# Joining the transposing transfers of a fused attention and highway layer, with the schedule made anew

## The chip, the cores and the metric

The kernel runs on one core of a Trainium2 chip. The metric is the device time of one execution in microseconds (us). The five engines are named as in the profile: PE (matmuls; PEld its weight loads), DVE, ACT, POOL, and SP, which here only issues DMA transfers. A name with a q (SPq, POOLq) is the engine's sequencer, which issues and waits.

## The reference

```python
# q, k, v: 8 batches, 12 heads, 448 rows, 64 columns, float32; tau = 0.1
q_n = q / (norm(q) + 1e-06);  k_n = k / (norm(k) + 1e-06)      # per row
scores = q_n @ k_n.T / tau
attn = softmax(scores)
x = (attn @ v), heads side by side                             # 3584 x 768
H = maximum(x @ w_h, 0);  T = sigmoid(x @ w_t + b_t)           # 768 x 768 weights
out = T * H + (1 - T) * x
```

## The kernel before

The work goes over 8 batches. Within one, the 12 heads are taken as 6 pairs (heads p and p + 6), so there are 48 pairs, numbered `s = 6 * b + p`. The 448 rows of a head are 3 x 128 main rows and a tail of 64. Operands of products are f16.

For each batch the main rows of q, k and v are loaded with a cast by POOL (`load_main`, `load_v`), the f32 tails by SP (`load_tails`). `square`, `tail_squares` and `folds` make the squared norms; `newton` makes their inverse roots (on ACT in batch 0, in seven small DVE steps later). `scaled` multiplies q and k of one pair by the roots into a buffer `qn`, on POOL (line 499); `qtnorm` and `ktnorm` scale the tails into `qtn` and `kb`.

The products need q and k with the 64 columns on the partitions, so `qn` is transposed into `qT`. In batches 0 to 3 `turn` does that with seven PE transposes and one eviction by DVE (line 547). In batches 4 to 7 (`BY_DMA`) it is a transposing DMA transfer that SP issues: one per pair, six 128 x 128 blocks (line 532). `turn_tails` does the same for the tails: one transfer of three blocks for q (`qtT`, line 555) and one of six for k (`kbT`, line 558).

`scores` makes the score products of a pair on PE (lines 600 and 614) and ACT takes their exponential (606, 618). `attend` multiplies with v (644, 648, 664), and DVE divides by the row sums (672, 674) into `x`, a buffer of one batch. v is cast into `vp` by `vcast` (626) and `vtcast` (632).

`ffn` is the highway layer, four tiles a batch: three of 128 x 2 rows and one half tile of the tails, in which the two halves of the 768 columns lie on the two halves of the partitions. x of a tile is transposed, in batches 1 to 6 by one transfer from SP for each tile (line 704). The products with both weights are lines 745 and 729, the gate is made by ACT (768, 769) and DVE (782, 787, 790), the last addition by POOL (line 795) and at the end by DVE. SP stores the result: one transfer of a full tile (805), two for the half tile, 64 rows of half the columns each (801).

The order is written out by hand. Every operation is put down with its engine, what it reads and what it writes; `ORDER` is the order in which all 1723 of them are issued, and so the order on each engine, and `SLOTS` says which buffer of a ring each new value takes. Nothing else schedules. `NR` gives the rings: four `qn`, four `qT`, three `xT`, four `os` (results that wait for their store).

DVE and POOL are kept apart by extra order: an operation that uses the port that both share is marked `port`. Such an operation on POOL waits for the last such one before it on DVE; those in `URGENT` are also waited for by the next one on DVE.

SP issues in order. Its transfers use eight completion marks in turn, so that a transfer also waits until the one eight before it has landed.

Of the kernel before, what the change touches and what calls it, by code (L numbers as in the profile page):

```python
# [9 lines left out]
FP16 = mybir.dt.float16  # L10
# [92 lines left out]
""".replace("\n", "")  # L103
)

URGENT = frozenset(
    int(n)
    for n in """
116 135 154 155 225 310 336 337 394 413 485 583 621 736 774 811 877 945 963 998 1080 1106 1140 1147 1166 1237
1268 1283 1298 1369 1387 1405 1440 1471 1553 1554 1571 1589 1590 1607 1608 1643 1691  # L110
""".split()
)


class Op:
# [801 lines left out]
```

## Time and profile before

| | |
|---|---|
| median of 3 runs (lowest to highest) | 275.48 us (273.61 to 279.13) |
| the profiled execution | 274.65 us |
| its span in the profile | 272.8 us |
| granted TensorE clock | 0.994 |
| DMA traffic | 43.13 MB in 104249 packets |

The span is what the profile shows from the first instruction to the last; the time of the execution is 1.85 us longer. Durations of single instructions come from that one execution. Of two instructions in a row on an engine, the second often starts about 0.1 us before the first ends, so summed durations exceed busy time by a few per cent.

### The profile page before, as it was taken

What the parts mean: (1) busy time and instruction counts of PE and PEld (TensorE: products, weight loads), DVE (VectorE), ACT (ScalarE), POOL (GpSimd) and SP (SyncE); (2) the same over time, 40 slices, a digit from 0 to 9 for tenths busy, and PEclk for the clock granted to TensorE, in tenths of its full rate; (3) what the DMA queues carried; (4) which work ended last, traced back from release to release, by engine and by line L of the source; (5) the groups of instructions that cost most, each with busy time, mean ns of one, the idle gap of its engine ahead of it and who ended that gap; (6) DMA issues with size and microseconds to landing.
All of it is one profiled execution on the core that took longest, in us unless ns stands there. A gap on an engine that the chain in (4) does not pass through costs nothing.

```text
span 272.8 us, 9106 instructions
## 1 busy us (share of the span) xinstructions
PE 243.6 (89%) x3783; PEld 163.2 (60%) x3783; DVE 198.2 (73%) x446; ACT 209.6 (77%) x312; POOL 159.1 (58%) x172
## 2 busy tenths in 40 slices
PE   0467898999999999999999897998899999999990
PEld 0235475766775676666656574665566767677650
DVE  6577989999989889976876778629853454446464
ACT  2479999879896998789689898797798995683120
POOL 5979656585584775576766564558667464300540
PEclk9999999999999999999999999999999999999997
DMA  7999999999859999996999989999795749620243
GB/s 131 221 192 191 180 207 202 186 194 198 105 78 176 209 164 119 150 171 128 210 157 151 173 191 181 143 190 222 173 167 86 116 124 191 204 90 2 60 178 113
DMA packets 104249, 43.13 MB, mean 158 GB/s; under 512 B 98064, under 2 KB 101136, under 8 KB 104208
## 3 DMA queue, kind: packets, MB, share of 16 engines
q0 software_dynamic: 38464, 16.32, 49.3%
q1 hardware_dynamic: 64512, 25.80, 48.7%
q8 instruction: 30, 0.49, 0.7%
q10 hardware_dynamic: 1232, 0.43, 0.6%
q14 instruction: 11, 0.09, 0.1%
HBM read 37.82 MB, written 11.01 MB: 179 GB/s over the span
## 4 chain that ended last, share of the span: by engine, by line
PE 53%; DVE 17%; DMA 14%; ACT 5%; POOL 3%; issue 3%; SPq 2%; POOLq 0%; ACTq 0%; DVEq 0%
PE pS L745 24%; PE pS L600 7%; PE pB L648 7%; PE pS L729 4%; DMA qT<-qn 4%; DMA qr<-in_q_dram 4%; DMA out_dram<-os 3%; PE pB L664 3%; PE pB L614 3%; PE pB L644 3%; DVE sq L374 2%; POOL qn L499 2%; DMA kr<-in_k_dram 2%; DVE f L388 2%; ACT E L606 2%
## 5 line engine op out<-in xcount | busy, mean ns | idle before, releaser
L606 ACT ACTIVATE E<-pS 128x896 f16<-128x896 f32 x144 | 128.5, 920 | 21.0 <-PE pS L600 18.0
L745 PEld LDWEIGHTS <-xT 64*128 64x128 f16 x1152 | 52.9, 94 | 33.6 <-issue 2.2
L795 POOL TENSOR_TENSOR os<-x,hm 128x768 f32<-128x768 f16 (+1 forms) x30 | 44.2, 1479 | 41.6 <-DVE hm L790 28.5
L745 PE MATMUL pS<-wt,xT 64*128 64x384 f16 x576 | 58.6, 323 | 0.6 <-DMA xT<-x 0.6
L745 PE MATMUL pS<-wh,xT 64*128 64x384 f16 x576 | 57.5, 323 | 0.0
L499 POOL TENSOR_TENSOR qn<-kr,rs 128x384 f16<-128x384 f16 x47 | 39.1, 841 | 30.4 <-DVE rd L672 10.4
L499 POOL TENSOR_TENSOR qn<-qr,rs 128x384 f16<-128x384 f16 x47 | 38.9, 832 | 22.9 <-DVE hm L790 8.3
L600 PE MATMUL pS<-qT 64*128 64x384 f16 x288 | 44.1, 327 | 3.8 <-DMA qT<-qn 1.7
L648 PE MATMUL pB<-vp,E 128*128 128x65 f16 x864 | 43.6, 194 | 0.0
L782 DVE SCALAR_TENSOR_TENSOR hm<-pS,x 128x768 f16<-128x768 f32 (+1 forms) x33 | 27.4, 833 | 19.8 <-PE pS L745 13.6
L648 PEld LDWEIGHTS <-E 128*128 128x128 f16 x864 | 38.5, 98 | 1.2 <-issue 0.7
L600 PEld LDWEIGHTS <-qT 64*128 64x128 f16 x576 | 23.2, 94 | 21.7 <-issue 7.8
L644 PE MATMUL pB<-vp,Et 128*128 128x130 f16 x144 | 32.0, 222 | 0.8 <-ACT Et L618 0.6
L769 ACT ACTIVATE tt<-pS 128x768 f16<-128x768 f32 x24 | 19.5, 813 | 16.3 <-PE pS L745 15.0
L618 ACT ACTIVATE Et<-pB 128x512 f16<-128x512 f32 x48 | 28.5, 603 | 2.9 <-PE pB L614 2.7
L674 DVE SCALAR_TENSOR_TENSOR x<-pB,rd 128x448 f16<-128x448 f32 x48 | 29.7, 620 | 1.1
L600 PE MATMUL pS<-qtT,qT 64*128 64x64 f16 x282 | 27.6, 189 | 0.0
L672 DVE RECIPROCAL rd<-pB 128x7 f32<-128x7 f32 x48 | 9.5, 200 | 22.7 <-PE pB L648 14.4
L280 PE MATMUL pB<-fill 128*128 128x384 f16 x40 | 9.6, 367 | 13.3 <-DVE fill L251 10.7
L626 ACT COPY vp<-vr 128x384 f16<-128x384 f16 x42 | 21.1, 515 | 0.0
L790 DVE TENSOR_TENSOR hm<-tt,hm 128x768 f16<-128x768 f16 (+1 forms) x32 | 18.3, 581 | 2.8 <-POOL os L795 2.6
L664 PE MATMUL pB<-vp,E 128*128 128x65 f16 x288 | 18.3, 194 | 0.2 <-DVE x L674 0.2
(95 smaller groups left out, 382.3 us busy)
## 6 DMA issues: line engine op xcount, KB each, us to landing
out_dram<-os SPq DMA_DIRECT2D x24, 384.0 KB, 3.7
vr<-in_v_dram POOLq DMA_DIRECT2D x8, 576.0 KB, 9.6
kr<-in_k_dram POOLq DMA_DIRECT2D x7, 576.0 KB, 9.8
qr<-in_q_dram POOLq DMA_DIRECT2D x7, 576.0 KB, 11.4
qt<-in_q_dram SPq DMA_DIRECT2D x16, 96.0 KB, 5.8
vt<-in_v_dram SPq DMA_DIRECT2D x16, 96.0 KB, 5.0
out_dram<-os SPq DMA_DIRECT2D x16, 96.0 KB, 2.4
kt<-in_k_dram SPq DMA_DIRECT2D x14, 96.0 KB, 4.9
```

What stands on the lines that cost most here:

```text
L499: return e.tensor_mul(R("qn", s)[:, t].rearrange("l c ab d -> l ab c d"), rows(t, b, p, p + 1)[:, :, 0, :].rearrange("l ab (c d) -> l ab c ...
L600: ins = nc.tensor.matmul(dst, lhsT=qT[ln, 384 + 128 * c : 512 + 128 * c], rhs=rhs, start=True, stop=True)
L606: return nc.scalar.activation(R("E", s)[:, c, :, 0:448], R("S", 3 * s + c)[:, :, 0:448], AF.Exp, scale=inv_tau)
L618: op("ACT", f"expt {s}", lambda: nc.scalar.activation(R("Et", s)[:, 64:576], R("B", ("S", s))[:, :], AF.Exp, scale=inv_tau), key + 3, r=[( ...
L626: return nc.vector.tensor_copy(dst, src) if b == 0 else nc.scalar.copy(dst, src)
L644: nc.tensor.matmul(U[:, 2 * c : 2 * c + 2, :].rearrange("p g e -> p (g e)"), lhsT=Et[:, 128 + 128 * c : 256 + 128 * c], rhs=vp[:, 6:8, :]. ...
L648: ins = nc.tensor.matmul(U[:, 2 * c + ab, :], lhsT=EF[:, j, 576 * ab + 128 * c : 576 * ab + 128 * c + 128], rhs=vp[:, 3 * ab + j, :], star ...
L664: ins = nc.tensor.matmul(U[:, 6, :], lhsT=lt, rhs=rh, start=(n == 0), stop=(n == 7))
L674: op("DVE", f"ev {s}", lambda: nc.vector.scalar_tensor_tensor(out=R("x", b)[:, :, D * p : D * p + D], in0=U_()[:, :, 0:D], scalar=0.0, in1 ...
L745: ins = nc.tensor.matmul(P[:, h, 0:MH], lhsT=lt, rhs=rh, start=(part == 0 and cc == (-1 if wi == 0 else 0)), stop=(part == 1 and cc == CC ...
L782: return nc.vector.scalar_tensor_tensor(out=o_, in0=i0, scalar=0.0, in1=xs, op0=ALU.max, op1=ALU.subtract)
L795: op(en, f"out{wd} {g}", lambda: eng.tensor_add(R("os", g)[:, 0:W], xall(), R("hm", g)[:, 0:W]), at + 0.1, r=[("gg", g), ("x", b)], w=[("o ...
```

## The change

The transposing transfers are joined. In batches 4 to 7, `qn` and `qT` hold two pairs, and one transfer of twelve blocks turns q and k of both. The scaled tails of q now lie behind those of k in `kb`, and one transfer of nine blocks turns both (`tT` in place of `qtT` and `kbT`). x of a batch is turned by two transfers, of twelve and nine blocks, in place of four. The two half stores of a tail tile become one, whose destination is written as 2 x 64 x 384. SP has 36 operations fewer (108 in place of 144).

The rings follow: two `qn` of two pairs each, three `qT` of two, two `xT` of two tiles, two `sq` in place of three. Order and slots are new lists throughout, so that every engine's order changes, the first loads included. In the list of POOL the small first loads of k and q come in another order, and the bias loads stand between them.

A set `MOVED` lists 131 operations that run on another engine than the one that the code names first: `pick` chooses. The moves by kind:

| operation | from | to | count |
|---|---|---|---|
| scaling of q and k (`scaled`) | POOL | DVE | 45 |
| last addition (`out`, `outh`) | POOL | DVE | 14 + 4 |
| scaling of q tails (`qtnorm`) | POOL | DVE | 5 |
| scaling of k tails (`ktnorm`) | DVE | POOL | 10 |
| cast of v (`vcast`) | ACT to DVE, DVE to ACT | | 20, 2 |
| cast of v tails (`vtcast`) | ACT | DVE | 4 |
| squares (`square`, `tail_squares`) | DVE to ACT, ACT to DVE | | 15, 6 |
| eviction after PE transposes (`cpT`) | DVE | ACT | 6 |

PE has the same instructions, in another order. The diff without the lists, shortened:

```diff
-    NR = dict(qr=3, kr=3, qt=2, kt=2, kb=2, vr=3, vt=2, vp=2, sq=3, f1=2, f2=2, n2=2, rs=3, qn=4,
-              qtn=2, qtT=2, qT=4, kbT=2, E=3, Et=3, rd=2, x=4, xT=3, tt=3, hm=3, os=4, S=3, B=2)
+    NR = dict(qr=3, kr=3, qt=2, kt=2, kb=2, vr=3, vt=2, vp=2, sq=2, f1=2, f2=2, n2=2, rs=3, qn=2,
+              qT=3, tT=2, E=3, Et=3, rd=2, x=4, xT=2, tt=3, hm=3, os=4, S=3, B=2)
...
-        kb=ring("kb", NR["kb"], [128, NP, 2, D], FP16),
+        kb=ring("kb", NR["kb"], [128, NP + 3, 2, D], FP16),
...
+        qn=ring("qn", NR["qn"], [128, 2, 2, NCH, 2, D], FP16),
+        tT=ring("tT", NR["tT"], [128, NP + 3, 128], FP16),
+        qT=ring("qT", NR["qT"], [128, 14, 128], FP16),
...
+        xT=ring("xT", NR["xT"], [128, 2 * CC, 128], FP16),
...
+    def pick(one, other):
+        return other if len(pl.ops) in MOVED else one
+    def product(eng, out_, a, c):
+        return (nc.vector if eng == "DVE" else nc.gpsimd).tensor_mul(out_, a, c)
+    def copied(eng, out_, a):
+        return nc.scalar.copy(out_, a) if eng == "ACT" else nc.vector.tensor_copy(out_, a)
+    def squared(eng, out_, a):
+        return nc.scalar.activation(out_, a, AF.Square) if eng == "ACT" else nc.vector.tensor_mul(out_, a, a)
...
     def scaled(t, b, p, key, eng):
         s = 6 * b + p
-        e = nc.vector if eng == "DVE" else nc.gpsimd
+        eng = pick(eng, "DVE")
...
         if b in BY_DMA:
-            op("SP", f"xd6 q {s}", lambda: nc.sync.dma_start(
-                R("qT", s)[:, 0:768].rearrange("p (c l) -> p c l", c=6), R("qn", s).rearrange("l t c ab d -> l (t c ab d)"),
-                transpose=True), key, r=[("qn", s)], w=[("qT", s)])
+            if p % 2 == 0:
+                m = s // 2
+                op("SP", f"xd12 q {m}", lambda: nc.sync.dma_start(
+                    R("qT", m)[:, 1:13, :], R("qn", m).rearrange("l x t c ab d -> l (x t c ab d)"),
+                    transpose=True), key, r=[("qn", m, 0), ("qn", m, 1)], w=[("qT", m, 0), ("qT", m, 1)])
             return
...
-            op("SP", f"xd3 t {b}", lambda: nc.sync.dma_start(
-                R("qtT", b)[:, :, :], R("qtn", b).rearrange("l j ab d -> l (j ab d)"), transpose=True), key,
-               r=[("qtn", b)], w=[("qtT", b)])
-            op("SP", f"xd6 k {b}", lambda: nc.sync.dma_start(
-                R("kbT", b)[:, :, :], R("kb", b).rearrange("l p ab d -> l (p ab d)"), transpose=True), key,
-               r=[("kb", b)], w=[("kbT", b)])
+            op("SP", f"xd9 t {b}", lambda: nc.sync.dma_start(
+                R("tT", b)[:, :, :], R("kb", b).rearrange("l p ab d -> l (p ab d)"), transpose=True), key,
+               r=[("kb", b, 0), ("kb", b, 1)], w=[("tT", b)])
...
-        rd = [("E", s), ("Et", s), ("vp", b, p), ("vp", b, 6), ("zE", min(s, 2)), ("zEt", min(s, 2))]
+        rd = [("E", s), ("Et", s), ("vp", b, p), ("vp", b, 6)] + [(z, n) for z in ("zE", "zEt") for n in range(3)]
...
         if 1 <= b < B - 1:
-            op("SP", f"xd{nb} {g}", lambda: nc.sync.dma_start(R("xT", g)[:, 0:nb, :], xall(), transpose=True), key,
-               r=[("x", b)], w=[("xT", g)])
+            if not i % 2:
+                hf = i // 2
+                nd = 12 - 3 * hf
+                op("SP", f"xd{nd} {b} {hf}", lambda: nc.sync.dma_start(
+                    R("xT", (b, hf))[:, 0:nd, :], R("x", b)[:, 4 * hf : 4 + 3 * hf, :].rearrange("l h m -> l (h m)"),
+                    transpose=True), key, r=[("x", b)], w=[("xT", (b, hf), 0), ("xT", (b, hf), 1)])
...
-        eng, en = (nc.vector, "DVE") if last else (nc.gpsimd, "POOL")
+        en = "DVE" if last else pick("POOL", "DVE")
+        eng = nc.vector if en == "DVE" else nc.gpsimd
...
-            for h in range(2):
-                op("SP", f"sth {g} {h}", lambda h=h: nc.sync.dma_start(
-                    rows_[384:448, MH * h : MH * h + MH], R("os", g)[64 * h : 64 * h + 64, 0:MH]), at + 0.4,
-                   r=[("os", g)], w=[("o", g)])
+            op("SP", f"sth {g}", lambda: nc.sync.dma_start(
+                rows_[384:448].rearrange("l (h m) -> h l m", h=2), R("os", g)[:, 0:MH]), at + 0.4,
+               r=[("os", g)], w=[("o", g)])
```

More of the change, by code (lines that the diff above doesn't have):

```diff
@@ L108 @@
     for n in """
-116 135 154 155 225 310 336 337 394 413 485 583 621 736 774 811 877 945 963 998 1080 1106 1140 1147 1166 1237
-1268 1283 1298 1369 1387 1405 1440 1471 1553 1554 1571 1589 1590 1607 1608 1643 1691
+117 154 225 257 317 336 392 482 598 617 649 663 678 688 728 748 766 855 927 968 986 1004 1080 1090 1147 1148
+1164 1183 1261 1286 1378 1379 1395 1396 1413 1414 1443 1457 1482 1521 1540 1575 1592
+""".split()
+)
+MOVED = frozenset(
+    int(n)
+    for n in """
[6 rows of a table added]
 """.split()
@@ L213 @@
         rs=ring("rs", NR["rs"], [128, 3, NN], FP32),
-        qn=ring("qn", NR["qn"], [128, 2, NCH, 2, D], FP16),
-        kbT=ring("kbT", NR["kbT"], [128, NP, 128], FP16),
-        qtn=ring("qtn", NR["qtn"], [128, 3, 2, D], FP16),
-        qtT=ring("qtT", NR["qtT"], [128, 3, 128], FP16),
-        qT=ring("qT", NR["qT"], [128, 896], FP16),
+        qn=ring("qn", NR["qn"], [128, 2, 2, NCH, 2, D], FP16),
+        tT=ring("tT", NR["tT"], [128, NP + 3, 128], FP16),
+        qT=ring("qT", NR["qT"], [128, 14, 128], FP16),
         E=ring("E", NR["E"], [128, NCH, 2, 512], FP16),
@@ L368, in square @@
         for t, eng in enumerate(engs):
+            eng = pick(eng, "DVE" if eng == "ACT" else "ACT")
             def fn(t=t, eng=eng):
@@ L371, in fn @@
                 d = R("sq", i)[:, g0:g1, :].rearrange("l (p a c) d -> l a p (c d)", a=4, c=NCH)[:, 2 * t : 2 * t + 2]
-                if eng == "ACT":
-                    return nc.scalar.activation(d, a, AF.Square)
-                return nc.vector.tensor_mul(d, a, a)
+                return squared(eng, d, a)
             op(eng, f"sq{p1 - p0} {b} {p0} {t}", fn, key,
-               r=[rowtok(t, b, p) for p in range(p0, p1)] + ([("tab", 0)] if eng == "ACT" else []), w=[("sq", i)], port=eng == "DVE")
+               r=[rowtok(t, b, p) for p in range(p0, p1)] + [("tab", 0)], w=[("sq", i)], port=eng == "DVE")
         if tails:
@@ L395, in tail_squares, with fn @@
     def tail_squares(b, i, key):
-        def fn(t):
+        def fn(t, eng):
             sq = R("sq", i)[:, 6 * t : 6 * t + 6].rearrange("l g d -> l (g d)")
             a = R("qt", b).rearrange("l ab p d -> l (ab p d)") if t == 0 else R("kt", b).rearrange("l p d -> l (p d)")
-            return nc.scalar.activation(sq, a, AF.Square)
+            return squared(eng, sq, a)
         for t in range(2):
-            op("ACT", f"sqt {b} {t}", lambda t=t: fn(t), key, r=[("qt", b) if t == 0 else ("kt", b)] + ([("tab", 0)] if b == 0 else []),
-               w=[("sq", i)])
+            eng = pick("ACT", "DVE")
+            op(eng, f"sqt {b} {t}", lambda t=t, eng=eng: fn(t, eng), key,
+               r=[("qt", b) if t == 0 else ("kt", b)] + ([("tab", 0)] if b == 0 else []), w=[("sq", i)], port=eng == "DVE")
     def square_tail(b, key):
@@ L505, in scaled, with fn @@
         op(eng, f"{'qk'[t]}n {s}", fn, key, r=[rowtok(t, b, p), ("rn", b, p)], u=[("rs", b)],
-           w=[("qn", s)], port=True)
+           w=[("qn", s // 2, s % 2)], port=True)
     def qtnorm(b, key):
-        op("POOL", f"qtn {b}", lambda: nc.gpsimd.tensor_mul(
-            R("qtn", b).rearrange("l j ab d -> l ab j d"), R("qt", b)[:, :, :, :],
+        eng = pick("POOL", "DVE")
+        op(eng, f"qtn {b}", lambda: product(
+            eng, R("kb", b)[:, NP : NP + 3].rearrange("l j ab d -> l ab j d"), R("qt", b)[:, :, :, :],
             rtails(b).unsqueeze(3).to_broadcast([128, 2, 3, D])), key, r=[("qt", b), ("rn", b, 6)],
-           u=[("rs", b)], w=[("qtn", b)], port=True)
+           u=[("rs", b)], w=[("kb", b, 1)], port=True)
     def ktnorm(b, key):
         for ab in range(2):
-            def fn(ab=ab):
+            eng = pick("DVE", "POOL")
+            def fn(ab=ab, eng=eng):
                 ln = slice(64 * ab, 64 * ab + 64)
-                return nc.vector.tensor_mul(R("kb", b)[ln, :, ab, :], R("kt", b)[ln, :, :],
+                return product(eng, R("kb", b)[ln, 0:NP, ab, :], R("kt", b)[ln, :, :],
                                             R("rs", b)[ln, 0, 6:12].unsqueeze(2).to_broadcast([64, NP, D]))
-            op("DVE", f"kb {b} {ab}", fn, key, r=[("kt", b), ("zkb", min(b, 1)), ("rn", b, 6)], u=[("rs", b)],
-               w=[("kb", b)], port=True)
+            op(eng, f"kb {b} {ab}", fn, key, r=[("kt", b), ("zkb", min(b, 1)), ("rn", b, 6)], u=[("rs", b)],
+               w=[("kb", b, 0)], port=True)
     tn = [0]
@@ L565, in fn @@
             for j in range(3):
-                ins = nc.tensor.transpose(T[:, 128 * j : 128 * j + 128], R("qtn", b)[:, j].rearrange("l ab d -> l (ab d)"), ident[:, :])
+                ins = nc.tensor.transpose(T[:, 128 * j : 128 * j + 128], R("kb", b)[:, NP + j].rearrange("l ab d -> l (ab d)"), ident[:, :])
             return ins
-        op("PE", f"tail3 {b}", fn, key, mode="F", r=[("qtn", b), ("id", 0)], w=[("B", ("T", ti))])
+        op("PE", f"tail3 {b}", fn, key, mode="F", r=[("kb", b, 1), ("id", 0)], w=[("B", ("T", ti))])
         op("DVE", f"cpt3 {b}", lambda: nc.vector.tensor_copy(
-            R("qtT", b).rearrange("p j q -> p (j q)"), R16(("T", ti))[:, 0:384]),
-           key, r=[("B", ("T", ti))], w=[("qtT", b)])
+            R("tT", b)[:, NP : NP + 3].rearrange("p j q -> p (j q)"), R16(("T", ti))[:, 0:384]),
+           key, r=[("B", ("T", ti))], w=[("tT", b)])
     def turn_first_tails(key):
@@ L586, in scores @@
         s = 6 * b + p
-        tok = [("qT", s), ("qtT", b) if s else ("qtT0", 0)]
+        tok = [("qT", s // 2, s % 2), ("tT", b) if s else ("qtT0", 0)]
+        z = s % 2
         def tails():
-            return R("qtT", b)[:, p // 2, 64 * (p % 2) : 64 * (p % 2) + 64] if s else qtT0[:, :]
+            return R("tT", b)[:, NP + p // 2, 64 * (p % 2) : 64 * (p % 2) + 64] if s else qtT0[:, :]
         for c in range(NCH):
             def fn(c=c):
-                S_, qT = R("S", 3 * s + c), R("qT", s)
+                S_, qT = R("S", 3 * s + c), R("qT", s // 2)[:, 1 + 6 * z : 7 + 6 * z].rearrange("p c l -> p (c l)")
                 for part in range(2):
@@ L610, in ft @@
         def ft():
-            qT, S_ = R("qT", s), R("B", ("S", s))
-            keys = R("kbT", b)[:, p] if b in BY_DMA else qT[:, 768:896]
-            for dst, rhs in ((S_[:, 0:64], tails()), (S_[:, 64:448], qT[:, 0:384]), (S_[:, 448:512], tails())):
+            S_ = R("B", ("S", s))
+            qT = R("qT", s // 2)[:, 1 + 6 * z : 4 + 6 * z].rearrange("p c l -> p (c l)")
+            keys = R("tT", b)[:, p] if b in BY_DMA else R("qT", s // 2)[:, 13 * z]
+            for dst, rhs in ((S_[:, 0:64], tails()), (S_[:, 64:448], qT), (S_[:, 448:512], tails())):
                 ins = nc.tensor.matmul(dst, lhsT=keys, rhs=rhs, start=True, stop=True)
             return ins
-        op("PE", f"qkt {s}", ft, key + 3, mode="F", r=tok + ([("kbT", b)] if b in BY_DMA else []), w=[("B", ("S", s))])
+        op("PE", f"qkt {s}", ft, key + 3, mode="F", r=tok, w=[("B", ("S", s))])
         op("ACT", f"expt {s}", lambda: nc.scalar.activation(
@@ L622, in vcast @@
     def vcast(b, p, key):
+        eng = pick(*(("DVE", "ACT") if b == 0 else ("ACT", "DVE")))
         def fn():
@@ L625, in fn @@
             dst = R("vp", b)[:, p, 0:6, 0:D].rearrange("l (ab c) d -> l ab c d", ab=2)
-            return nc.vector.tensor_copy(dst, src) if b == 0 else nc.scalar.copy(dst, src)
-        op("DVE" if b == 0 else "ACT", f"vc {b} {p}", fn, key, r=[("vr", b), ("zvp", min(b, 1))], w=[("vp", b, p)], port=b == 0)
+            return copied(eng, dst, src)
+        op(eng, f"vc {b} {p}", fn, key, r=[("vr", b), ("zvp", min(b, 1))], w=[("vp", b, p)], port=eng == "DVE")
     def vtcast(b, key):
         for ab in range(2):
-            op("ACT", f"vtc {b} {ab}", lambda ab=ab: nc.scalar.copy(
-                R("vp", b)[64 * ab : 64 * ab + 64, :, 6 + ab, 0:D], R("vt", b)[64 * ab : 64 * ab + 64, :, :]),
-               key, r=[("vt", b), ("zvp", min(b, 1))], w=[("vp", b, 6)])
+            eng = pick("ACT", "DVE")
+            op(eng, f"vtc {b} {ab}", lambda ab=ab, eng=eng: copied(
+                eng, R("vp", b)[64 * ab : 64 * ab + 64, :, 6 + ab, 0:D], R("vt", b)[64 * ab : 64 * ab + 64, :, :]),
+               key, r=[("vt", b), ("zvp", min(b, 1))], w=[("vp", b, 6)], port=eng == "DVE")
     def attend(b, p, key):
@@ L714, in ffn @@
             op("DVE", f"cpx{nb} {g}", lambda: nc.vector.tensor_copy(
-                R("xT", g)[:, 0:nb].rearrange("p c l -> p (c l)"), R16(("T", ti))[:, 0 : 128 * nb]), key,
-               r=[("B", ("T", ti))], w=[("xT", g)])
+                xTg().rearrange("p c l -> p (c l)"), R16(("T", ti))[:, 0 : 128 * nb]), key,
+               r=[("B", ("T", ti))], w=[("xT", (b, i // 2), i % 2)])
         n = 0
@@ L733, in mm @@
             def mm(wi, w_, lo, hi, part):
-                P, xT = R(*bank_of(g, wi, False)), R("xT", g)
+                P, xT = R(*bank_of(g, wi, False)), xTg()
                 held = None
@@ L759, in ffn @@
                    (lambda w_=w_, wi=wi, lo=lo, hi=hi, part=part: mm(wi, w_, lo, hi, part)), at, mode=("C" if tail else "T"),
-                   r=[("xT", g), (wn, 0), ("bth", 0)] + ([("P0", g, wi, j - 1)] if j else []),
+                   r=[("xT", (b, i // 2), i % 2), (wn, 0), ("bth", 0)] + ([("P0", g, wi, j - 1)] if j else []),
                    w=[("Pd", g, wi), ("P0", g, wi, j)], u=[bank])
```

49 lines of the change are left out of this document (26 added, 23 removed), and 141 rows, old and new, of tables (MOVED, ORDER).

## The prediction

> **What bounds the kernel now.** I read the page first, then the busy time by stages, then the chain of waits, then the DMA queue's own waits.
>
> ```profile
> span 272.8 us, 9106 instructions
> PE 243.6 (89%) x3783; PEld 163.2 (60%) x3783; DVE 198.2 (73%) x446; ACT 209.6 (77%) x312; POOL 159.1 (58%) x172
> ```
>
> No engine is full over the whole span, so the stages have to be looked at one by one. In the next view each row is a stretch of the span, then its length, then busy time (and count) of PE, weight loads, DVE, ACT and POOL; the share after PEclk counts waiting packets of both DMA queues.
>
> ```profile
> 0.00:18.00 18.00, 5.74 (x38) 3.15 (x40) 12.69 (x47) 7.61 (x14) 13.65 (x22) 1.00 1.20 180
> 18.00:43.00 25.00, 21.05 (x341) 14.40 (x336) 21.16 (x52) 23.07 (x35) 18.09 (x23) 1.00 1.42 193
> 43.00:105.00 62.00, 60.97 (x988) 42.05 (x986) 57.15 (x125) 56.10 (x85) 38.60 (x43) 1.00 1.14 162
> 105.00:131.00 26.00, 25.62 (x419) 17.08 (x416) 21.20 (x45) 21.26 (x33) 17.73 (x19) 1.00 1.03 156
> 131.00:192.00 61.00, 56.85 (x899) 37.58 (x898) 44.51 (x93) 52.31 (x79) 37.12 (x38) 1.00 1.19 176
> 192.00:249.00 57.00, 55.97 (x907) 38.58 (x906) 28.26 (x66) 45.82 (x66) 26.45 (x25) 1.00 0.65 138
> 249.00:272.80 23.80, 17.41 (x213) 10.34 (x207) 13.23 (x24) 3.41 (x5) 7.42 (x5) 0.93 0.29 101
> ```
>
> Four regimes stand there. Up to 18 us the first loads and norms set the time. From 18 to 105 us PE, ACT and DVE are all near 90% (82.0, 79.2 and 78.3 of 87 us): three engines hand work to each other and none has room. From 131 to 192 us PE idles 4.15 us although ACT and DVE have more room than before. At the end 6.4 us pass in which PE has little or nothing. What rules the third regime is told by the chain of waits (start, length, what):
>
> ```profile
> 137.14 0.83 POOL qn L499
> ...
> 158.29 4.36 DMA qT<-qn
> ...
> 164.46 5.93 DMA qT<-qn
> ...
> 172.52 2.12 SPq L704
> ...
> 175.42 6.75 DMA out_dram<-os
> ...
> 182.30 1.65 POOL os L795
> ```
>
> The chain leaves PE: it goes through POOL's scaling of q and k, the transposing transfers and the stores, all issued by SP in one order. SP itself is close to full there; its timeline has instruction after instruction without a gap:
>
> ```profile
> 150.14 2.33 SPq L558 DMA_TRANSPOSE kbT<-kb  x1
> 152.56 2.22 SPq L532 DMA_TRANSPOSE qT<-qn  x1
> 154.87 0.63 SPq L337 DMA_DIRECT2D vt<-in_v_dram  x1
> ```
>
> **The change, part by part.**
>
> *Fewer, larger transposing transfers.* 24 of q and k become 12, 24 of x become 12, 8 of tails become 4. The rows of the lines (durations are SP's issue, minimum/median/maximum in ns; the last line belongs to L532):
>
> ```profile
> L555 SPq DMA_TRANSPOSE qtT<-qtn x4: 1200/1212/1262, 115.7 to 214.5; - x4
> L558 SPq DMA_TRANSPOSE kbT<-kb x4: 1237/1754/2327, 123.2 to 205.6; - x4
> L532 SPq DMA_TRANSPOSE qT<-qn x24: 1210/1250/3177, 120.8 to 230.1; - x24
> DMA to landing us min/median/max: 2.7/3.6/9.1
> ```
>
> Three blocks (L555) and six (L558, L532) take the same shortest issue, 1.20 and 1.21 us, so the issue seems to be per transfer. Twelve blocks are not in the trace: bounds are 1.25 us (no dependence) and 2.5 us (double the six). I take 1.25, the nearer reading of 1.20 against 1.21. SP is then freed of 28 x 1.25 = 35 us, or of nothing. Against it, a pair now waits for its neighbour: both pairs' scaled q and k must be there, and the landing of twelve blocks lies between 2.7 us and twice that, 5.4; by the new order PE has work for 5 to 9 us between the issue and the first score matmul that reads it, so most of it stays covered, and where it does not, the score matmul (and all behind it on PE) is late.
>
> What it is worth is bounded by the stage: PE's idle time between 105 and 249 us is 0.4 + 4.15 + 1.0 = 5.6 us. I take -3, since ACT, at 52.3 of 61 us in the worst stretch, also gains work (next part). Bounds: -5.6, and +3 where the pair's later start shows, about one median landing.
>
> *Work moved between engines.* Beside the joins, 131 operations change engine. POOL gives 45 scalings, 18 gate additions and 5 tail scalings to DVE and takes 10 key-tail scalings; DVE gives 13 squares and 6 evictions to ACT and takes 18 net casts of v.
>
> ```profile
> L499 POOL TENSOR_TENSOR qn<-kr,rs 128x384 f16<-128x384 f16 x47 | 39.1, 841 | 30.4 <-DVE rd L672 10.4 <-DVE kb L518 7.7 <-DVE f L390 2.4
> L470 DVE TENSOR_TENSOR qn<-first,first_rs 128x384 f16<-128x384 f32 x2 | 1.1, 550 | 0.0
> L795 POOL TENSOR_TENSOR os<-x,hm 128x768 f32<-128x768 f16 x23 | 38.0, 1653 | 41.1 <-DVE hm L790 28.1 <-DMA out_dram<-os 7.6 <-DVE f L390 3.0
> L795 DVE TENSOR_TENSOR os<-x,hm 128x768 f32<-128x768 f16 x1 | 1.0, 957 | 0.0
> L626 ACT COPY vp<-vr 128x384 f16<-128x384 f16 x42 | 21.1, 515 | 0.0
> L626 DVE COPY vp<-vr 128x384 f16<-128x384 f16 x6 | 2.0, 325 | 0.0
> L373 ACT ACTIVATE sq<-kr 128x1152 f16<-128x1152 f16 x1 | 1.1, 1147 | 0.0
> L374 DVE TENSOR_TENSOR sq<-kr 128x1152 f16<-128x1152 f16 x14 | 12.0, 859 | 0.1
> L547 DVE COPY qT<-pB 128x896 f16<-128x896 f16 x24 | 14.5, 612 | 4.9 <-PE pB L543 2.5 <-ACT E L606 2.3
> L518 DVE TENSOR_TENSOR kb<-kt,rs 64x384 f16<-64x384 f32 x16 | 9.8, 613 | 0.4
> ```
>
> DVE gains 45 x 0.55 + 14 x 0.96 + 4 x 0.56 + 5 x 0.55 + 18 x 0.33, some 49 us, plus about 3 for a few tail squares and tail casts, and loses 10 x 0.61 + 13 x 0.86 + 6 x 0.61, 21 us: +31, from 198 to about 229. ACT gains 13 x 1.15 and 6 x about 0.92 (its 896-wide exponentials), and loses 18 x 0.52 and some smaller ones: +6. POOL loses about 60. The scaling from f16 on DVE is not in the trace; 0.55 is the row with an f32 source, and nothing below the 0.33 of the same-sized cast is likely, so DVE's gain is 21 to 31 us.
>
> Where it falls matters. Going through the new order up to the attention of pair 17, which the trace reaches at 105 us, ACT has 5 us more to do and DVE 4 to 5 more, in the regime where both stand near 90%. If their shares stay, 18 to 105 us grows by 5 / 0.91 = 5.5 us; if the two fill their idle time, it grows by nothing. POOL's waits (the idle of 30 us before L499, most of it ended by DVE) become shorter when DVE does both steps, which speaks for the lower half: I take +4, bounds 0 and +6. Later DVE has room (44.5 of 61), and ACT's extra 1 us lies inside it.
>
> *New order at the start.* The small first loads of k for pairs 1 and 2 now stand seventh on POOL, behind two bias loads. The first pair's norms move ahead of the wait that held them:
>
> ```profile
> 8.58 0.84 ACT L373 ACTIVATE sq<-kr 128x768 f16<-128x768 f16 x1 [2.04 <-DMA kr<-in_k_dram]
> 9.87 0.41 DVE L462 TENSOR_TENSOR first_fa<-first_sq 128x480 f16<-128x480 f16 x1 [2.65 <-ACT first_sq L456]
> ```
>
> That is worth at most the 2.65 us DVE waits there. But DVE now does the square of k for pairs 1 and 2 and a fold before it scales the first key tails, and that square waits for the later load (three to four issues of about 0.75 us). The first pair comes perhaps 1.5 us sooner, pairs 1 to 5 about 1 later, and DVE does six of their scalings. I take +1, bounds -1.5 and +2.
>
> *The half stores joined.* The last fences show the end: two stretches (all full stores, then the two last halves), the packets of the last 24 us, and SP's last two issues with their landing.
>
> ```profile
> 268.60:269.80 1.20, 0.00 (x0) 0.00 (x0) 0.34 (x1) 0.00 (x0) 0.00 (x0) 0.84 0.84 328
> 269.80:271.40 1.60, 0.00 (x0) 0.00 (x0) 0.00 (x0) 0.00 (x0) 0.00 (x0) 0.50 0.55 123
> DMA packets 1042, 2.39 MB, mean 101 GB/s; under 512 B 144, under 2 KB 400, under 8 KB 1040
> 268.97 1.11 SPq L801 DMA_DIRECT2D out_dram<-os  x2
> DMA to landing us min/median/max: 2.1/2.2/2.2
> ```
>
> The nine stores of that window leave 144 tiny packets, 16 each: one mark per engine, with 64 or 128 rows dealt over sixteen. The joined store is written as 2 x 64 x 384, so its outermost dimension has two entries. If it is dealt by that dimension, two engines carry it. The two last halves cost 0.55 x 16 x 1.60 = 14.1 engine-us, 7.0 us on two engines; at the rate of the full stores (0.84 x 16 x 1.20 = 16.1 engine-us for twice the bytes) 4.0 us. Today they land 2.2 us after the second issue, 2.7 after the first, some 0.6 of it transfer. The joined one would land 1.6 + 4.0 to 7.0 = 5.6 to 8.6 us after its issue: +2.9 to +5.9 at the very end, since it is SP's last instruction in the new order as well. Over sixteen engines it is 1.6 + 0.9, so -0.2. No store here has such a shape; I take two engines, because rows are dealt whole by the outer dimension in every store seen, and the middle, +4.4. The seven earlier ones hold two engines for 4 to 7 us each, and a transfer issued behind one waits for its share on those two; by the new order one of them (of batch 2, with a transfer of x of batch 5 about 3 us of PE work behind it) meets a consumer 5 us after that: +1, bounds 0 and +3.
>
> The Trainium skill, "DMA: Bandwidth & Descriptors", section "Rules for kernel authors", speaks for the join: two transfers to disjoint partition halves serialize, so one 128-partition transfer is to be used; by that alone the end would be -0.2 and the sum 277.5. The same page, section "Why a DMA increments its semaphore by 16 and not by 1", says that the number of engines is the largest up to 16 that divides the slowest dimension of both access patterns, here 2 and 128, so two engines; by that it is the term taken. No store in this trace shows a count under sixteen.
>
> **The sum.** The profiled execution took 274.65 us (span 272.8 and 1.85 around it), 0.3% under the median 275.48. +1 (start) +4 (load of ACT and DVE) -3 (SP and transposes) +1 (stores on the way) +4.4 (last store) = +7.4: 282.05 us, 2.4% over the median.
>
> **The rivals.**
> 1. *Faster: SP and POOL were the bottleneck.* The chain above speaks for it: between 137 and 184 us it runs in SP, POOL and their transfers. If all 5.6 us of PE's idle time from 105 to 249 go, the first pair is 1.5 us sooner, DVE's added work fits its gaps and the store goes over sixteen engines: 274.65 - 5.6 - 1.5 - 0.2 = 267.4. Against it: ACT's 90% up to 105 us, with more to do.
> 2. *No change: the joins do what they say, the last store takes it back.* -5.6 + 4.4 and nothing else: 273.5. For it speaks that PE's work is the same, instruction for instruction.
> 3. *Much slower: three engines coupled.* DVE rises to about 84% beside ACT and PE. Its place is 18 to 249 us; it decides from where DVE's share exceeds ACT's. If PE's idle time there (3.95 + 1.0 + 5.6 = 10.5 us) doubles, and the last store costs 4.4: 289.6.
>
> **How the numbers follow.** Forecast 0.45, its own range 277 to 287 by its bounds; rival 1 0.32, rival 2 0.10, rival 3 0.13. A measurement of this kernel tells about 2% from no change: 270.0 and 281.0. Of the forecast's 0.45 some seven tenths lie above 281.0: slower 0.32 + 0.13 = 0.45. Faster: nearly all of rival 1, 0.30. The rest, 0.25, is within. The range 267 to 289 leaves out the outer half of rivals 1 and 3.
>
> **What would show it.** Two engines: 2 tiny packets for a joined store instead of 16, and landing of 5.6 us or more; wrong if it lands in under 3. Issue: the L560 transfers (twelve blocks) near 1.25 us. Load: DVE near 229 and ACT near 216 us busy, and PE idle more than 5 us in the stretch that ends with pair 17. SP: the chain between 130 and 190 us back in PE or ACT. If PE's idle time from 18 us to the last pair falls below 7 us, the forecast is wrong and rival 1 right.

## The result and the profile after

The changed kernel takes 286.52 us (median of 4 runs, 285.17 to 288.04), the kernel before 275.62 us (273.61 to 279.13) beside it: a ratio of 1.0422, 95% interval 1.0337 to 1.0508. That is slower by 11.6 us at the ratio; the forecast was 7.4 us slower. Here and below, medians are of all executions, and ratios leave out those more than 1.5% above the fastest of the same kernel.

The page of the changed kernel gives span and busy time; its row of PE by 40 slices and the row of the granted clock belong to the same part:

```profile
span 286.3 us, 9041 instructions
PE 248.7 (87%) x3783; PEld 166.2 (58%) x3783; DVE 221.8 (77%) x511; ACT 215.1 (75%) x305; POOL 101.6 (35%) x114
PE   4477879999999799999994789899599999999950
PEclk9879999999999799999999799999989999999995
```

The engines' loads moved as the diff says: DVE +24 us, ACT +5.5, POOL -57. PE has the same 3783 matmuls and needs 5.1 us more for them, of which 3.1 fall in the first 18 us (next table), and it is idle for 37.6 us in place of 29.2. In the 40 slices a slice of low clock goes with, or comes right behind, each clear hole in PE: the 7 at the 14th place stands in both rows, the 4 at the 22nd place is followed by the 7 of the clock at the 23rd, the 5 at the 29th by the 8 at the 30th. So these holes cost their own length and some clock behind them.

The same stretches as before (length; then busy time and count of PE, weight loads, DVE, ACT, POOL; clock, DMA share, GB/s):

```profile
0.00:18.00 18.00, 8.86 (x40) 3.82 (x41) 12.94 (x46) 6.33 (x12) 12.92 (x21) 0.83 1.22 180
18.00:43.00 25.00, 19.57 (x320) 13.65 (x319) 22.99 (x58) 24.68 (x38) 13.57 (x15) 0.99 1.42 193
43.00:105.00 62.00, 59.23 (x912) 39.84 (x910) 55.04 (x126) 55.80 (x77) 29.91 (x32) 0.97 1.13 157
105.00:131.00 26.00, 26.00 (x435) 18.16 (x435) 24.88 (x57) 24.63 (x36) 9.61 (x11) 1.00 1.03 175
131.00:192.00 61.00, 54.06 (x851) 36.66 (x846) 46.08 (x104) 49.49 (x69) 21.93 (x23) 0.97 1.11 162
192.00:249.00 57.00, 54.04 (x854) 36.59 (x852) 37.62 (x86) 43.23 (x62) 11.13 (x11) 0.97 0.70 137
249.00:286.30 37.30, 26.91 (x396) 17.49 (x392) 22.25 (x41) 10.90 (x16) 2.55 (x2) 0.89 0.24 82
```

Up to 131 us little is lost: by 130 us, 23 of the 48 pairs have reached their division in both kernels. From 131 to 249 us PE idles 9.9 us (6.94 and 2.96) where it was 5.2, and behind 249 us 10.4 where it was 6.4. Most of the 9.9 us is PE waiting for DVE, 8.4 us in all, and DVE waits for a store before that (who <- for whom: us in total, times, longest):

```profile
DVE os L837 <- DMA out_dram<-os: 9.1, 2, 5.7
PE pS L786 <- DVE hm L823: 5.3, 1, 5.3
PE pS L630 <- DVE hm L823: 3.1, 2, 3.0
```

L837 is the last addition, which DVE now does in 20 of the 32 tiles. It writes into `os`, so the store that read this buffer must have landed. Both times that is a joined half store, L842; the view of its line gives its issues, and under those who waited for it:

```profile
L842 SPq DMA_DIRECT2D out_dram<-os x8: 517/580/682, 144.4 to 278.6; - x8
  DVE os L837: 9.1, 2
```

The first joined store is issued at 144.4 us, the addition that needs its buffer starts at 156.2, and PE goes on at 159.0: that is the hole near 155 us. The chain of waits (start, length, what) shows the second hole from inside; SP issued that joined store at 196.70:

```profile
196.70 6.48 DMA out_dram<-os
203.27 0.96 DVE os L837
204.23 0.67 DVE f L410
205.17 0.88 DVE hm L823
206.09 0.78 PE pS L630 x8
```

That these stores are late because they are joined is a reading so far; the experiments decide. The DMA view of the last 24 us, and SP's last issue:

```profile
DMA packets 1111, 2.57 MB, mean 106 GB/s; under 512 B 86, under 2 KB 470, under 8 KB 1110
out_dram<-os SPq DMA_DIRECT2D x5, 384.0 KB, 2.3
out_dram<-os SPq DMA_DIRECT2D x3, 192.0 KB
```

```profile
278.55 0.52 SPq L842 DMA_DIRECT2D out_dram<-os  x1
```

Five full stores leave 5 x 16 tiny packets, so the three joined ones leave 86 - 80 = 6, two each: two engines carry them. The share of the DMA engines agrees: from 280 to 283 us, when nothing but the last store runs, it is 0.13, which is 2 of 16. From the issue of the last one at 278.55 to the end of the span pass 7.75 us; before, from 268.97 to 272.8, 3.8.

### The profile page after: what moved, and what is told of

The parts are those of the page before. It is cut to its first block, busy times and chain, and to the rows that moved or that the text cites. A ratio compares the mean times of both kernels' runs of the same rounds, so it can differ in the third digit from the quotient of the medians.

```text
span 286.3 us, 9041 instructions
## 1 busy us (share of the span) xinstructions
PE 248.7 (87%) x3783; PEld 166.2 (58%) x3783; DVE 221.8 (77%) x511; ACT 215.1 (75%) x305; POOL 101.6 (35%) x114
## 4 chain that ended last, share of the span: by engine, by line
PE 60%; ACT 10%; DMA 9%; DVE 9%; SPq 4%; issue 3%; POOL 2%; DVEq 0%; ACTq 0%
PE pS L786 27%; PE pS L630 8%; PE pB L682 7%; ACT E L636 5%; PE pS L770 4%; PE pB L698 3%; DMA kt<-in_k_dram 3%; PE pB L645 3%; PE pB L678 3%; DMA out_dram<-os 2%; PE pB L570 2%; DMA xT<-x 2%; SPq L560 2%; DMA qr<-in_q_dram 2%; DVE x L708 2%
## 5 line engine op out<-in xcount | busy, mean ns | idle before, releaser
L786 PEld LDWEIGHTS <-xT 64*128 64x128 f16 x1152 | 54.2, 95 | 34.5 <-issue 1.7
L786 PE MATMUL pS<-wh,xT 64*128 64x384 f16 x576 | 56.3, 323 | 0.0
L682 PE MATMUL pB<-vp,E 128*128 128x65 f16 x864 | 44.5, 195 | 0.0
L253 POOL TENSOR_TENSOR qn<-qr,rs 128x384 f16<-128x384 f16 x25 | 21.9, 877 | 54.4 <-DVE qn L253 24.8
L837 POOL TENSOR_TENSOR os<-x,hm 128x768 f32<-128x768 f16 (+1 forms) x12 | 17.4, 1456 | 51.8 <-DVE hm L831 37.3
L253 POOL TENSOR_TENSOR qn<-kr,rs 128x384 f16<-128x384 f16 x24 | 19.8, 827 | 35.1 <-PE pB L573 6.7
L630 PE MATMUL pS<-tT,qT 64*128 64x64 f16 x282 | 27.8, 191 | 0.0
L837 DVE TENSOR_TENSOR os<-x,hm 128x768 f32<-128x768 f16 (+1 forms) x20 | 17.7, 887 | 9.3 <-DMA out_dram<-os 9.1
L698 PE MATMUL pB<-vp,E 128*128 128x65 f16 x288 | 18.3, 195 | 0.1
L678 PEld LDWEIGHTS <-Et 128*128 128x128 f16 x144 | 14.1, 98 | 6.0 <-issue 3.9
L302 PE MATMUL pB<-fill 128*128 128x384 f16 x40 | 10.4, 408 | 7.1 <-DVE fill L273 4.2
```

Of the source, the lines that this page charges most:

```text
L253: return (nc.vector if eng == "DVE" else nc.gpsimd).tensor_mul(out_, a, c)
L630: ins = nc.tensor.matmul(dst, lhsT=qT[ln, 384 + 128 * c : 512 + 128 * c], rhs=rhs, start=True, stop=True)
L678: nc.tensor.matmul(U[:, 2 * c : 2 * c + 2, :].rearrange("p g e -> p (g e)"), lhsT=Et[:, 128 + 128 * c : 256 + 128 * c], rhs=vp[:, 6:8, :]. ...
L682: ins = nc.tensor.matmul(U[:, 2 * c + ab, :], lhsT=EF[:, j, 576 * ab + 128 * c : 576 * ab + 128 * c + 128], rhs=vp[:, 3 * ab + j, :], star ...
L698: ins = nc.tensor.matmul(U[:, 6, :], lhsT=lt, rhs=rh, start=(n == 0), stop=(n == 7))
L786: ins = nc.tensor.matmul(P[:, h, 0:MH], lhsT=lt, rhs=rh, start=(part == 0 and cc == (-1 if wi == 0 else 0)), stop=(part == 1 and cc == CC ...
```

## The experiments

Theory E: the joined store is the loss, because two engines carry 192 KB, so that it lands late and the share that other transfers have on those two engines waits. Rivals: the load moved to DVE and ACT, the larger transposes (a pair waits for its neighbour), the smaller rings, or the store's place in SP's queue. Ratios are to the kernel before, run beside each, with a median of 276.66 to 277.31 us; microseconds in brackets are worked out from ratio and median.

### Two half stores again, the rest of the change kept

```diff
-            op("SP", f"sth {g}", lambda: nc.sync.dma_start(
-                rows_[384:448].rearrange("l (h m) -> h l m", h=2), R("os", g)[:, 0:MH]), at + 0.4,
+            def both():
+                for h in range(2):
+                    ins = nc.sync.dma_start(
+                        rows_[384:448, MH * h : MH * h + MH], R("os", g)[64 * h : 64 * h + 64, 0:MH])
+                return ins
+            op("SP", f"sth {g}", both, at + 0.4,
```

> The changed kernel with one part undone: the half tile is stored by two transfers of 64 rows again, issued one after the other in the place of the joined one. Theory A (the joined store runs on two of sixteen engines, and both the end and the middle pay for it): the 4.5 us at the end come back and the waits behind it in the middle (os buffers 9.1 us of DVE's waits, loads that land in 6.7 us behind it) go too, 277 to 280 us. Theory B (the end alone pays; the middle is slow for other reasons): 282, minus 4.5. Theory C (the store is not the cause): 286.

Measured: 274.8 us (273.11 to 278.76), ratio 0.993, interval 0.989 to 0.997. The same kernel, a second time on another chip:

> The changed kernel with two half stores in the joined one's place, once more, so that the next three runs have it beside them on the same chip. Theory E (two busy DMA engines are the whole loss): 272 to 277 us, a ratio to before of 0.985 to 1.0, as in the first run of it (274.8 us, 0.993). If that first gain was an accident of one chip: 1.0 or above.

Measured: 276.19 us, ratio 0.9995, interval 0.9955 to 1.0036. With two half stores the change lies between 1.1% faster and 0.4% slower, so all of its loss sits in the store. From the page and the stages of the first run:

```profile
span 271.2 us, 9051 instructions
PE 245.2 (90%) x3783; PEld 165.4 (61%) x3783; DVE 222.4 (82%) x511; ACT 214.8 (79%) x305; POOL 101.7 (38%) x114
```

```profile
18.00:43.00 25.00, 20.31 (x326) 14.09 (x324) 23.01 (x56) 24.67 (x38) 13.56 (x15) 0.96 1.42 193
43.00:105.00 62.00, 59.17 (x941) 40.56 (x939) 56.40 (x129) 57.06 (x80) 30.05 (x32) 1.00 1.17 163
131.00:192.00 61.00, 58.44 (x962) 40.44 (x960) 52.89 (x119) 54.20 (x76) 22.19 (x24) 1.00 1.12 178
192.00:249.00 57.00, 56.08 (x912) 38.94 (x906) 37.61 (x82) 44.09 (x62) 10.30 (x10) 1.00 0.55 121
```

The loads are those of the changed kernel; DVE at 82% and ACT at 79% are bearable. From 131 to 249 us PE idles 3.5 us in place of 9.9. DVE's waits for an `os` buffer from 140 to 249 us are 4.5 us in place of 9.1; they don't vanish, since the half stores there land up to 8.8 us after their issue; the first joined one took 11.1.

### The joined store alone, in the kernel before

```diff
-                    rows_[384:448, MH * h : MH * h + MH], R("os", g)[64 * h : 64 * h + 64, 0:MH])
+                    rows_[384:448].rearrange("l (h m) -> h l m", h=2), R("os", g)[:, 0:MH])   # once for both halves
```

> The kernel before with one part of the change done: the half tile is stored by one transfer of 2 x 64 x 384, in the place of the later of the two. Order, engines and transposes are those of before. Theory A: +4.5 at the end and 1 to 4 us more on the way, 281 to 284 us. Theory B: +4 to +4.5, 279.5 to 280. Theory C: 275.5. The store should leave 2 tiny packets in place of 16.

Measured: 290.39 us (287.76 to 291.53), ratio 1.0484, interval 1.0415 to 1.0553. Eight stores written otherwise cost 13.4 us at the ratio: undone they give the loss back, done alone they make it.

### The last one, and the seven before it

The same edit for the last half tile alone (`g == 4 * B - 1`), and for all but the last.

> The kernel before, with the joined store for the very last half tile alone; the seven others stay two transfers. Theory A1 (the last store costs its landing, the rest of the 13 us comes from stores on the way): +4 to +4.7 us on before. Theory A2 (the end is most of it): +10 or more.

> The kernel before, with the joined store for the seven half tiles ahead of the last, which stays two transfers: the other part of the same cost. Theory A1: +7 to +10 us, with PE waiting for transposing transfers that stand behind a store on the same two engines. The prediction's own term for this was +1.

Measured: the last alone 282.57 us, ratio 1.0211, interval 1.0113 to 1.031 (+5.8 us); the seven alone 286.9 us, 1.0325, interval 1.0178 to 1.0473 (+9.0 us). Neither interval holds 1, but both are wide. Both together make 14.8, near the 13.4 of all eight. In the first, SP issues the last store at 274.96 and the span ends at 282.6, 7.6 us later, as in the changed kernel. (That it reaches this store 6 us later than the kernel before, though nothing is changed ahead of it, is scatter: this execution took 284.41 us, the longest of four, and those of the kernel before beside it range from 274.83 to 281.42.)

```profile
span 282.6 us, 9105 instructions
```

```profile
274.96 0.64 SPq L803 DMA_DIRECT2D out_dram<-os  x1
```

What the seven do is seen in PE's waits from 140 to 249 us (us in total, times, longest); first the run, whose PE lines are the first three, then the kernel before:

```profile
PE pS L746 <- DMA xT<-x: 4.3, 2, 2.4
PE pS L600 <- DMA qtT<-qtn: 3.7, 1, 3.7
PE pB L614 <- DMA qT<-qn: 1.5, 1, 1.5
```

```profile
PE pS L600 <- DMA qT<-qn: 1.7, 2, 1.0
PE pB L614 <- DMA qtT<-qtn: 0.7, 1, 0.7
```

PE waits for transposing transfers 9.5 us in place of 2.4. Those transfers are no other than before. As single executions scatter, more of them are needed: the same waits are 4.5 us in the run with only the last store joined and 3.8 in the run with 128 x 384 stores (next section), but 11.1 with all eight joined. The median landing of the transposes of q and k is 3.6, 3.6 and 3.3 us in the three executions without two-engine stores there, 4.0 with seven and 6.4 with all eight. So these waits make some 5 to 7 of the 9.0 us. Three of the four waits, 7.6 us, end 8 to 9 us after a joined store behind which SP next issued transposes of the awaited kind (stores at 170.15, 200.76 and 220.90; PE goes on at 178.24, 209.62 and 229.17). The fourth, 1.9 us at 144 us, has no joined store in the 30 us ahead of it.

### One store on sixteen engines, and one from another queue

Again in the kernel before, one store for both halves. In the first, its destination is written as 128 x 384, rows and halves in turns; by that the tail rows of the output stand in another order. In the second, POOL issues the 2 x 64 x 384 store.

```diff
+                    rows_[384:448].rearrange("l (h m) -> (l h) m", h=2), R("os", g)[:, 0:MH])          # first
+                op("POOL", f"sth {g} {h}", lambda ...: nc.gpsimd.dma_start(
+                    rows_[384:448].rearrange("l (h m) -> h l m", h=2), R("os", g)[:, 0:MH])            # second
```

> The kernel before, with one store for each half tile of the same bytes to the same region in rows of the same 1536 bytes, but written as 128 x 384, the halves put down in turns; so the tail rows of the output are permuted. Theory A (the number of engines is the cost, and the outermost dimension sets it): 16 tiny packets, landing near 2.5 us, time that of before or up to 1 us less. If a single transfer of this size is itself the cost: as slow as with 2 x 64 x 384, +13.

> The kernel before, with the joined store of 2 x 64 x 384 issued by POOL in place of SP, at the same point of the order. Theory Q (what hurts on the way is that transposes and loads of SP stand in SP's own queue behind the store on two engines): the middle recovers even if POOL's store also uses two engines, +1 to +6 us on before, the last landing and some POOL time included. Theory E (two busy engines hurt every transfer, whatever queue): +10 or more. If POOL deals the same shape over sixteen engines: -0.5 to +2.

Measured: the first 277.39 us (273.91 to 278.27), ratio 1.0005, interval 0.9953 to 1.0058; the second 290.22 us, 1.0473, interval 1.0368 to 1.0579. The joined store among the DMA issues (count, size, us to landing) of the first, the packets and the full and joined stores of the first from 249 us on, and the joined store of the second:

```profile
out_dram<-os SPq DMA_DIRECT2D x8, 192.0 KB, 2.5
```

```profile
DMA packets 1012, 2.42 MB, mean 91 GB/s; under 512 B 112, under 2 KB 368, under 8 KB 1008
out_dram<-os SPq DMA_DIRECT2D x5, 384.0 KB, 3.1
out_dram<-os SPq DMA_DIRECT2D x2, 192.0 KB, 2.0
```

```profile
out_dram<-os POOLq DMA_DIRECT2D x8, 192.0 KB, 7.8
```

The first is as joined as the store of the change: one instruction, the same 192 KB, the same place on SP. It leaves 16 tiny packets (112 for seven stores), lands in 2.5 us and costs nothing measurable. So joining isn't the fault, the count of engines is. And the queue isn't either: from POOL the store lands in 7.8 us, with a DMA share of 0.12 while only the last one runs (again 2 of 16), and the kernel is as slow as with SP. PE's waits from 140 to 249 us for the transposes, which SP still issues, are 8.6 us there. The rival in which the store blocks what stands behind it on SP's own queue falls by that: two busy engines hold up SP's transposes whoever issued the store.

### The joined transposes, with the joined store in place

q and k of a pair by two transfers of six blocks, in the changed kernel; then, in another run, x of a batch by four transfers.

```diff
-                    R("qT", m)[:, 1:13, :], R("qn", m).rearrange("l x t c ab d -> l (x t c ab d)"),
+                            R("qT", m)[:, 1 + 6 * z : 7 + 6 * z, :], R("qn", m)[:, z].rearrange("l t c ab d -> l (t c ab d)"),   # z = 0, 1
```

> The changed kernel with one part undone: q and k of two pairs are turned by two transfers of six blocks, issued back to back in the place of the one of twelve. Theory D (the long transfers block SP, whose issue of twelve blocks took up to 4.3 us, and deliver late): faster, 281 to 284 us. Theory of the prediction (the issue is paid per transfer, joining frees SP): slower by up to 12 issues of 1.25 us where SP is full, 287 to 292 us. If SP is not what holds the middle up: 286.

> The changed kernel with one part undone: x of a batch is turned by four transfers, two and two back to back in the places of the joined ones. Theory D (long transfers block SP; x's took up to 4.5 us to issue and 13 to land): faster, 282 to 285 us, as the first tile's x is there sooner. Theory of the prediction: slower, 287 to 291 us. If it is hidden anyway: 286.

Measured: pairs apart 290.77 us, 1.0517, interval 1.0464 to 1.0571; x apart 288.27 us, 1.043, interval 1.0382 to 1.0478. Neither gives anything back, so the larger transposes aren't the loss. DVE's waits for an `os` buffer stay, 8.9 and 8.7 us from 140 us on. Whether joined pairs gain the 4 us by which the medians differ from 286.52 stays unclear here: the intervals touch.

### The same with two half stores

> The changed kernel with two half stores, and q and k of a pair by two six-block transposes each instead of one twelve-block one. With the joined store in place, taking the pairs apart had cost 4 us (290.77 against 286.52). Theory A (joined pairs help by themselves: 12 issues on SP fewer, each over 1.2 us): 2 to 4 us above the run with two stores alone, 277 to 279 us. Theory B (they help only where two busy engines hold up every transfer, so that fewer transfers meet fewer waits): within 1 us of the run with two stores alone, 274 to 276 us.

> The changed kernel with two half stores, and q and k of a pair and x of a batch by as many transposes as before: of the change there remain the joined tails, the smaller rings, and the new order. Theory A (the joined transposes are what gains): 277 to 280 us, level with before or 1% above it. Theory B (the new order and the joined tails are what gains, the joins only move issue time on a queue that has slack): 273 to 276 us, level with the run with two stores alone.

Measured: pairs apart 277.83 us, 0.9992, interval 0.9942 to 1.0041, which is level with the 0.9995 of the joined pairs; pairs and x apart 281.55 us, 1.0109, interval 1.0059 to 1.016. Twelve issues less for q and k are worth nothing measurable (the intervals leave room for some 2 us); the theory that they gain by themselves is not borne out. For x some 1% (3 us) speaks for the join: with x taken apart on top of the pairs the intervals don't touch, but they come close, and the ten executions with both apart scatter from 277.59 to 285.31 us; x alone was not run with two half stores. The DMA issues (count, median us to landing) show what a join pays, first the run with two half stores, then that with pairs apart, then that with pairs and x apart (its profiled execution is the longest of the ten):

```profile
xT<-x SPq DMA_TRANSPOSE x12, 4.4
qT<-qn SPq DMA_TRANSPOSE x12, 5.4
```

```profile
xT<-x SPq DMA_TRANSPOSE x12, 4.3
qT<-qn SPq DMA_TRANSPOSE x24, 4.0
```

```profile
xT<-x SPq DMA_TRANSPOSE x24, 3.0
qT<-qn SPq DMA_TRANSPOSE x24, 3.8
```

Half as many transfers, each landing 1.3 to 1.6 us later: for q and k the time comes out level. Why x would come out ahead is not shown.

A further run gave the transposed x a third tile, against SP's wait for the full ring of two. It changes part of the output, for a reason that was not found, so its time is no evidence; that wait, and with it a version clearly better than both kernels, stays open.

## Why the prediction was right or wrong

The direction was right and the size 4 us short. That it came so near is in part luck, as two errors of opposite sign met: without the stores the change was put at +2 us and is worth 0 to -2, and the stores were put at +5.4 us and cost 12 to 14. To place the terms, the division by the row sums of pair 5 and of the last pair (the last figures before the semicolon are first and last start) in the kernel before, in the run with two half stores, and in the changed kernel (last pair only):

```profile
L672 DVE RECIPROCAL rd<-pB x1: 205/205/205, 43.3 to 43.3; 128x7 f32<-128x7 f32 x1
L672 DVE RECIPROCAL rd<-pB x2: 201/204/206, 247.0 to 248.7; 128x7 f32<-128x7 f32 x2
```

```profile
L706 DVE RECIPROCAL rd<-pB x1: 198/198/198, 43.1 to 43.1; 128x7 f32<-128x7 f32 x1
L706 DVE RECIPROCAL rd<-pB x3: 205/206/206, 243.1 to 246.2; 128x7 f32<-128x7 f32 x3
```

```profile
L706 DVE RECIPROCAL rd<-pB x2: 205/206/206, 256.7 to 257.7; 128x7 f32<-128x7 f32 x2
```

- **Start, +1.** Pair 5 comes at 43.1 us in place of 43.3: about nothing, inside its bounds. The way there was another: the first division comes at 29.6 us in place of 28.3, where the first pair was expected 1.5 us sooner, and the pairs behind it catch up.
- **Load of ACT and DVE, +4.** With two half stores PE idles 7.5 us from 18 to 105 us in place of 5.0: +2.5, inside 0 to +6. DVE came to 222 us (forecast 229) and ACT to 215 (216), so the forecast of DVE was too high. Part of the +2.5 may have another cause than load, which is not shown: in the changed kernel the transpose of x waits for PE, by the code for a free one of the two `xT`, and the loads of k stand behind it on SP, as its timeline shows near 89 us. In the kernel before SP stands there for almost as long (from 77.1 to 86.9 us), and its load of k goes out at 88.64.

```profile
78.68 0.60 SPq L359 DMA_DIRECT2D vt<-in_v_dram  x1
89.28 1.31 SPq L744 DMA_TRANSPOSE xT<-x  x1
90.68 1.28 SPq L353 DMA_DIRECT2D kt<-in_k_dram  x2
```

- **SP and transposes, -3.** With two half stores PE idles 3.5 us from 105 to 249 us in place of 5.6, and the last pair comes 2.5 us sooner. The size fits that one execution; the ratios of two sets of ten runs leave 0 to -2 us for the whole change without its store, in place of +1 -3 +4 = +2. The step "issue is per transfer" was nearly right for the shortest issue, as the changed kernel's row says: twelve blocks take 1.41 us (1.28 with two half stores), where 1.25 was taken and 2.5 was the other bound. But the median is 1.70 us, against 1.25 for six blocks before, so the joins free SP of less than was taken.

```profile
L560 SPq DMA_TRANSPOSE qT<-qn x12: 1414/1704/4277, 126.3 to 234.7; - x12
```

- **Last store, +4.4.** Right: 7.75 us from its issue to the end in place of 3.8, and +5.8 us (interval 1.13% to 3.1%, 3.1 to 8.6 us) where it is the only edit. Two tiny packets, as by the section "Why a DMA increments its semaphore by 16 and not by 1" of "DMA: Bandwidth & Descriptors" in the Trainium skill; this trace agrees with it, and where the slowest dimension was 128, as in the 128 x 384 store, there were 16 of them and it landed in 2.5 us.
- **Stores on the way, +1.** This is the term that was mis-sized. The seven cost +9.0 us alone in the kernel before (interval 4.9 to 13.1 us), where 0 to +3 was the range. In the changed kernel, by the ratios with and without the joined store, both store terms make 11.8 to 13.6 us; less the last one's 4 to 6 that leaves 6 to 10. The step that failed is the search for one consumer: the prediction followed one transposing transfer, that of x behind the store of batch 2, and asked if PE's work covers it. In the kernel before, transposes of three kinds behind three of the stores came late, 1.5 to 3.7 us each for PE. In the changed kernel PE waits for transposes only 0.8 us from 140 to 249 us; there the consumer is the store's own buffer, for which the prediction had no term. DVE, which the change gave most of the last additions, waits 9.1 us for `os` in place of 4.5, PE waits 8.4 us for DVE in place of 3.4, and behind the two longer holes some clock is lost as well. That these parts make up the whole 6 to 10 us is not shown.

The other marks that the prediction named: PE idles 8.2 us from 18 to 105 us in the changed kernel (over 5 was forecast), its idle time from 18 us to the last pair is 18 us (below 7 would have spoken for rival 1), and the chain from 130 to 190 us is in PE and ACT up to 152 us, then in SP, its transfers and DVE, and from 180 us in PE.

Rival 1 is right in that ACT and DVE can carry the added load (with two half stores the chain lies 71% in PE, 9% in DVE and 6% in ACT), but not in its price: 0 to 2 us were there to be gained, not 7. Rival 2, no change because the last store takes back what the joins give, fell with the seven earlier ones. Rival 3's 289.6 us was nearest in time but not in cause: the coupling of DVE, ACT and PE is no loss by the run with two half stores. The section "Rules for kernel authors" of the same page, by which two transfers to disjoint partition halves should be one, would have given 277.5; the 128 x 384 store agrees that the joined form costs nothing on sixteen engines (and gains nothing measurable, 1.0005), while the 2 x 64 x 384 form is what was built.

## What to carry to other kernels

Before two transfers are joined, look at the outermost dimension of the joined pattern on both sides: one of two entries confined the transfer to two engines here, and for a store that SP issues the tiny packets of its completion, counted in the DMA view, tell it at once. Cost such a transfer not by one consumer but by two things: what is issued behind it over all engines, and who waits for the buffer that it reads. A join of transfers saves issue time and pays in landing time; for q and k here the time came out level. And compare one execution's waits with more than one execution of the other kernel.

## What the hardware showed that was not expected

- Seven 192 KB stores on two engines each cost 9.0 us of 277. PE's waits from 140 to 249 us for transposes that were not touched are 9.5 us, against 2.4 to 4.5 in three executions whose stores there run on sixteen engines.
- The same store issued by POOL lands in 7.8 us and costs the same 4.7%: a queue of its own doesn't make it faster.
- A hole in PE can cost more than its length. In the changed kernel PE stood 5.3 us until 159.0 and 3.0 us until 206.1; at each start the granted clock is near 0.5 and is back at 1.00 only 3 to 4 us later. With seven stores joined, a wait of 3.7 us until 229.2 is followed by the same, and one of 2.4 us until 178.2 is not. But a hole of 2 us at 95 us in the changed kernel is, so what decides is not shown. From 18 us on, the matmuls of the changed kernel take 239.8 us of busy time against 235.4 with two half stores, where no such drop occurs between 43 and 249 us.
